# Dynamic convolution and two dense layers on one core: 24 shared 4 KB places and a written-out order of issue

## The chip, the cores and the metric

The kernel runs on one core of one Trainium2 chip. The metric is the device time of one execution in microseconds (us). Engines are named as in the profile: PE multiplies matrices (PEld loads its weights), DVE, ACT and POOL work on tiles elementwise, SP only issues DMAs. SBUF is the on-chip memory of the tiles, PSUM the small one that PE writes.

## The reference

```python
w = softmax(weight_gen over its 7 taps)                       # 2 x 4096 x 8 x 7
x1[s, h, :] = sum over k of w[s, h, k] * x[s + k - 6, h, :]   # 8 heads of 24 columns
h = x1 @ w_in;  g = h / (1 + exp(-h));  x2 = g @ w_out        # 8192x192 -> 2048 -> 192
h = x2 @ w_in2
g = (a0 + a1*h + a2*h^2 + a3*h^3) / (1 + |b0|*|h| + |b1|*h^2 + 1e-6)
out = g @ w_out2
```

All of it in float32. The weights arrive as 8-byte floats and are turned into 4-byte ones on the chip, with integer operations on their two words.

## The kernel before

**Tiling.** The 8192 tokens are cut into 16 blocks of 512. A block goes through the convolution (`attention`, four token groups j), a transpose on PE (T), the first layer in eight units u of 256 hidden columns (`unit1`), a step between the layers (`between`), the second layer in eight units (`unit2`), and `finish`, which transposes back and stores.

**Two halves for each operand.** PE's fast float32 format keeps fewer bits, so each operand is split into a rounded half (hi) and the rest (lo = value - hi). A group of ten 512-column matmuls makes one hidden tile `h` (A in layer 1, B in layer 2: `mm1`, L544), another group of ten adds the unit to the output (C, D: `mm2`, L565 to L569). The second operand halves are `xh`, `xl` (inputs of a layer), `g1h`, `g1l`, `g2h`, `g2l` (activated hidden tiles).

**Chains of a unit.** Layer 1: A, then on ACT the silu in place (S, L581) and the rounded half (H, L585), then on DVE the lo subtraction (L, L589). Layer 2: B, then on ACT two readers of the PSUM tile (U, L626 and V, L630), then on DVE u (L636) and w (L639), which read the PSUM tile too, and Y (L645); on ACT a logarithm and a sigmoid (N, L650 and G, L653), which make the reciprocal; on DVE the product g (L656); the rounded half h (L243 on ACT, L245 on POOL or L247 on DVE) and the lo subtraction l (L666, on DVE or POOL), which read and write SBUF alone. S, N and G need three different function tables on ACT, so a change among them costs an ACT_TABLE_LOAD.

**PSUM** holds two `h` tiles (also used by T and by the transpose back, FT), and the two accumulators. A group A or B starts when the tile two before it has been read for the last time: by L in layer 1, by w in layer 2.

**Order.** Every operation has a number in the table KEYS (one table for blocks 0, 1 and 15, one for the rest, moved by 72 a block); `Plan.order` sorts all 2922 of them, and each engine executes its own in that order, one after another. ENGINES picks another engine for some. SBUF tiles come from pools with a fixed number of buffers, taken in turn: five `y`, five `t` (both serve as raw and decoded weights during the start), two each of `g1h`, `g1l`, `g2h`, `g2l`, one of each other. In the convolution, M multiplies 7 taps by their weights, p, r and a add them up, AD copies a part of the result by DMA (L493), and `between` swaps two halves by DMA.

Of the kernel before, what the change touches and what calls it, by code (L numbers as in the profile page):

```python
# [17 lines left out]
P = 128  # L18
J = 64
JB = 4  # L20
# [16 lines left out]
PERIOD = 72.0  # L37
KEYS = """
    q0O0l:-3113.02 q0O2l:-2632.43 q0B0l:-2598.9 q0O2a:-2459.82 q0A0l:-2443.19 q0O6l:-2381.11 q0A0a:-2309.74
    q0O21:-2304.16 q0A01:-2174.4 q0O0a:-2166.02 q0B0a:-2153.38 q0O22:-2115.39 q0B01:-2103.18 q0B02:-1964.9  # L40
    q0B03:-1964.37 q0O23:-1909.62 cn:-1901.54 q0B04:-1854.81 s0l:-1796.69 q0O01:-1778.45 q0O24:-1772.97 q0O02:-1754.69
    q0O2h:-1739.82 q0B0d:-1736.66 q0A02:-1725.96 q0A1l:-1702.71 q0B0h:-1658.16 q0O03:-1644.78 q0O04:-1637.27
    q0A03:-1622.71 q0O0h:-1589.04 q0O6a:-1548.27 q0A04:-1539.2 q0A3l:-1532.67 q0O2x:-1506.98 q0A0h:-1485.47
    q0O61:-1471.06 q0O62:-1222.76 s0m:-1222.04 q0O63:-1184.06 q0O64:-1181.21 q0A0x:-1178.74 q0B1l:-1155.86
    q0O3l:-1152.08 zX:-1141.9 q0O6h:-1137.28 q0O0x:-1127.08 q0O6x:-1123.86 q0A1a:-1119.13 q0O3a:-1106.14
    q0A3a:-1087.37 q0A11:-1077.61 q0A31:-1051.29 q0O31:-1041.27 q0O1l:-1030.01 q0B0x:-1018.44 s0e:-1007.59
    q0B1a:-1005.54 q0A32:-994.85 s0n:-994.421 q0O32:-983.167 q0O1a:-945.552 q0A12:-913.372 q0A33:-900.533
    q0A13:-897.059 q0A34:-892.163 q0B11:-885.891 q0A14:-877.139 zM0:-874.91 q0O11:-866.459 zp0:-861.802 q0B12:-857.071
# [36 lines left out]
    q1O44:27.349 H5:27.354 yL0:28.011 zB2:28.845 q1O5x:29.2 L5:29.276 zU0:31.816 zu0:33.193 A7:34.231 q1O1x:34.79
    zV2:35.354 C5:37.242 S7:37.852 H7:38.496 q1O4h:38.505 zw0:40.456 C6:40.558 zU2:41.599 zV0:42.24 zY2:42.469
# [71 lines left out]
def table(text, kind):  # L158
    return {n: kind(v) for n, v in (e.split(":") for e in text.split())}
# [602 lines left out]
```

## Time and profile before

| what | value |
|---|---|
| median of 3 runs | 1366.06 us (1366.05 to 1366.27) |
| profiled execution, first to last instruction (span) | 1361.5 us |
| the runs' median less that span | 4.56 us |
| busy: PE, ACT, DVE, POOL | 91%, 88%, 84%, 34% |

The span is read as a start (decoding weights, first blocks), a steady part in which a block takes 77.8 us, and an end in which the last block has nothing to overlap with. A busy time counts instructions that overlap once.

### The profile page before, as it was taken

To read this page: it belongs to the slowest core of one execution; us is meant where nothing else is said; L and a number is where in the kernel's file an instruction comes from. 1 tells how busy PE (TensorE), PEld (TensorE's weight loads), DVE (VectorE), ACT (ScalarE), POOL (GpSimd) and SP (SyncE) were. 2 spreads that over 40 slices of the span, in tenths; PEclk is the share of its full clock that TensorE was granted. 3 is DMA by queue.
4 is the path that set the end of the run, shared out by engine and by line. 5 is a ranking of instruction groups with operands and counts; after the bars stand their busy time and mean duration, and the time that the engine had idled before them with its cause. 6 is when DMAs were issued, how large, how long until landed. Compare 5 with 4: busy or idle time off the path is not lost.

```text
span 1361.5 us, 14596 instructions
## 1 busy us (share of the span) xinstructions
PE 1243.2 (91%) x5440; PEld 990.5 (73%) x5440; DVE 1147.1 (84%) x1128; ACT 1192.4 (88%) x1129; POOL 468.5 (34%) x260
## 2 busy tenths in 40 slices
PE   0269899999999999999999999999999999999986
PEld 0147678777777877777877877787787777777764
DVE  5988888798889888788887998888888888878896
ACT  2375999989899998989999898989999898999996
POOL 0013534343524335252534425253443525211111
PEclk9989999999999999999999999999999999999999
DMA  6641011001011100101010100101010010000000
GB/s 182 185 144 56 14 43 37 20 0 37 20 51 40 37 20 2 36 20 37 20 37 20 49 34 8 37 20 37 20 37 20 1 37 20 5 20 0 20 1 24
DMA packets 26855, 49.20 MB, mean 36 GB/s; under 512 B 10916, under 2 KB 17186, under 8 KB 26784
## 3 DMA queue, kind: packets, MB, share of 16 engines
q1 hardware_dynamic: 26784, 48.27, 11.8%
q8 instruction: 43, 0.70, 0.2%
q14 instruction: 28, 0.23, 0.1%
HBM read 31.86 MB, written 8.01 MB: 29 GB/s over the span
## 4 chain that ended last, share of the span: by engine, by line
ACT 50%; PE 27%; DVE 12%; issue 7%; DMA 2%; SPq 0%; POOLq 0%; POOL 0%; ACTq 0%; DVEq 0%
PE h L544 17%; ACT y L650 7%; ACT L581 6%; ACT t L626 6%; ACT h L581 6%; ACT y L653 6%; ACT g1h L585 5%; ACT y L630 5%; ACT L650 4%; DVE g1l L589 4%; ACT L653 3%; PE acc L569 2%; PE acc L565 2%; PE acc L568 2%; PE acc L566 2%
## 5 line engine op out<-in xcount | busy, mean ns | idle before, releaser
L544 PE MATMUL h<-xh,wa 128*128 128x512 f32 x1024 | 332.1, 406 | 49.2 <-DVE g1l L589 32.5
L544 PEld LDWEIGHTS h<-xh,wa 128*128 128x128 f32 x1024 | 184.6, 190 | 127.1 <-DVE g1l L589 56.3
L589 DVE TENSOR_TENSOR g1l<-h,g1h 128x1024 fp32r<-128x1024 f32 x128 | 156.5, 1224 | 117.1 <-ACT g1h L585 115.9
L464 POOL TENSOR_TENSOR pr<-xw,aw 128x1344 f32<-128x1344 f32 x56 | 176.2, 3146 | 208.5 <-DVE ao L483 205.2
L245 POOL TENSOR_SCALAR g2h<-t 128x1024 fp32r<-128x1024 f32 x77 | 94.0, 1221 | 353.7 <-PE acc L567 254.8
L544 PE MATMUL h<-xl,wa 128*128 128x512 f32 x512 | 202.3, 395 | 0.9 <-DVE xl L521 0.8
L544 PE MATMUL h<-xh,wb 128*128 128x512 f32 x512 | 202.1, 395 | 0.0
L544 PE MATMUL h<-xl,wb 128*128 128x512 f32 x512 | 201.5, 394 | 0.0
L656 DVE SCALAR_TENSOR_TENSOR t<-t,a_sb,y 128x1024 f32<-128x1024 f32 x128 | 166.1, 1301 | 18.7 <-ACT y L653 18.7
L626 ACT ACTIVATE t<-h,a_sb 128x1024 f32<-128x1024 f32 x128 | 153.7, 1201 | 27.2 <-PE h L544 26.2
L581 ACT ACTIVATE h<-h 128x1024 f32<-128x1024 f32 x128 | 129.2, 1010 | 52.0 <-PE h L544 41.9
L645 DVE SCALAR_TENSOR_TENSOR y<-y,b_sb 128x1024 f32<-128x1024 f32 x128 | 168.2, 1314 | 7.6 <-ACT y L630 4.8
L639 DVE SCALAR_TENSOR_TENSOR t<-t,a_sb,h 128x1024 f32<-128x1024 f32 x128 | 163.7, 1279 | 2.9
L636 DVE TENSOR_TENSOR t<-t,h 128x1024 f32<-128x1024 f32 x128 | 155.6, 1216 | 11.0 <-ACT y L630 5.2
L630 ACT ACTIVATE y<-h,b_sb 128x1024 f32<-128x1024 f32 x128 | 141.7, 1107 | 8.5 <-PE h L544 7.0
L650 ACT ACTIVATE y<-y,c_sb 128x1024 f32<-128x1024 f32 x128 | 142.5, 1148 | 2.8 <-DVE y L645 1.8
L666 DVE TENSOR_TENSOR g2l<-t,g2h 128x1024 fp32r<-128x1024 f32 x92 | 139.8, 1522 | 2.6 <-POOL g2h L245 2.5
L585 ACT ACTIVATE g1h<-h 128x1024 fp32r<-128x1024 f32 x128 | 131.1, 1025 | 4.7 <-PE acc L567 1.3
L666 POOL TENSOR_TENSOR g2l<-t,g2h 128x1024 fp32r<-128x1024 f32 x36 | 89.5, 2487 | 131.5 <-DVE g2h L247 130.2
L653 ACT ACTIVATE y<-y 128x1024 f32<-128x1024 f32 x128 | 130.4, 1056 | 0.7
L544 PEld LDWEIGHTS h<-xl,wa 128*128 128x128 f32 x512 | 97.4, 190 | 23.7 <-DVE xl L521 2.3
L544 PEld LDWEIGHTS h<-xh,wb 128*128 128x128 f32 x512 | 97.4, 190 | 21.4
(94 smaller groups left out, 2452.8 us busy)
## 6 DMA issues: line engine op xcount, KB each, us to landing
xw<-in_x_dram SPq DMA_DIRECT2D x14, 960.0 KB, 5.1
raw<-in_moe_w_out_dram SPq DMA_DIRECT2D x16, 384.0 KB, 4.1
out_dram<-of SPq DMA_DIRECT2D x16, 384.0 KB, 2.3
raw<-in_moe_w_in_dram SPq DMA_DIRECT2D x8, 512.0 KB, 5.7
e<-e SPq DMA_DIRECT2D x32, 128.0 KB, 2.3
raw<-in_moe_w_in_dram SPq DMA_DIRECT2D x8, 256.0 KB, 6.1
dup<-dec SPq DMA_DIRECT2D x16, 128.0 KB, 2.3
ao<-ao SPq DMA_DIRECT2D x16, 128.0 KB, 2.3
```

What stands on the lines that cost most here:

```text
L464: e.tensor_tensor(out=p.rearrange("p k (h g) -> p k h g", g=G), in0=st[xw][:, j:j + K, :].rearrange("p k (h g) -> p k h g", g=G), in1=weig ...
L544: pe.matmul(out=h[:, i], lhsT=w[:, f], rhs=xx, start=(n == 0), stop=(n == len(terms) - 1))
L581: act.activation(out=st[hb], in_=st[hb], func=AF.Silu)
L585: act.activation(out=t, in_=st[hb], func=AF.Copy)
L589: dve.tensor_tensor(out=t, in0=st[hb], in1=st[gh].bitcast(F32), op=ALU.subtract)
L626: act.activation(out=q, in_=st[hb], func=AF.Identity, scale=a_sb[:, 3:4], bias=a_sb[:, 2:3])
L630: act.activation(out=q, in_=st[hb], func=AF.Abs, scale=b_sb[:, 1:2])
L645: dve.scalar_tensor_tensor(out=st[y], in0=st[y], scalar=b_sb[:, 0:1], in1=st[y], op0=ALU.add, op1=ALU.mult)
L650: act.activation(out=st[y], in_=st[y], func=AF.Ln, scale=c_sb[:, 0:1], bias=1e-6)
L653: act.activation(out=st[y], in_=st[y], func=AF.Sigmoid, scale=-1.0)
L656: dve.scalar_tensor_tensor(out=st[t], in0=st[t], scalar=a_sb[:, 0:1], in1=st[y], op0=ALU.add, op1=ALU.mult)
L666: e.tensor_tensor(out=q, in0=st[t], in1=st[gh].bitcast(F32), op=ALU.subtract)
```

## The change

1. **Places.** The pools of `y`, `t`, `g1h`, `g1l`, `g2h`, `g2l`, `xh`, `xl`, `ao` and `of` (24 buffers in all) become 24 single buffers named a to x. The order names the place of each new tile (`H1.5:r`).
2. **Order.** KEYS and ENGINES go; ORDER lists all 2922 operations, each block with an order of its own, with the choice of engine (`@1`).
3. **Engines.** By that list: of the 128 lo subtractions of layer 2, 84 run on POOL (36 before); of the 128 rounded halves 9 run on ACT (30 before), 32 on DVE (21) and 87 on POOL (77); of the copies out of PSUM in `finish` DVE makes 15 of 16 FE (none before) and 7 of 16 FC (1), ACT the others; of the 192 additions p, r, a 141 run on POOL (58 before), of the 64 products M 43 (56 before).
4. **AD** becomes a copy on POOL (12 blocks) or ACT (2), and stays a DMA in 2.
5. ACT and DVE read one PSUM tile one after the other; the list gives the turn per unit (V, U, u, w or U, V, u, w in 120 of 128 units, V behind u in the others; before 125). The arithmetic is the same.

```diff
-BUFS = dict(
-    h=2, acc0=1, acc1=1, xw=1, aw=2, pr=1, ao=1, xh0=1, xl0=1, xh1=1, xl1=1, of=1,
-    g1h=2, g1l=2, y=5, t=5, g2h=2, g2l=2,
-)
...
+    r0.3@1 L1.2:x A2.2 G7.0 a0.3:i M2.3 g7.0 B0.1 S2.2 H2.2:r p2.3@1 C1.2 U0.1:b L2.2:t V0.1:v q1O72 r2.3@1 A3.2
...
+SLOTS = "abcdefghijklmnopqrstuvwx"
+SHARED = {"y", "t", "g1h", "g1l", "g2h", "g2l", "ao", "of", "xh0", "xl0", "xh1", "xl1"}
+OWN = dict(xw=1, pr=1, aw=2)
...
+            for v in bufs:
+                if v[0] in SHARED and v not in self.slot:
+                    self.slot[v] = slot
+            fn(engines[names[int(e or 0)]])
...
-    def new(tag, shape, dt=F32, name=None):
-        return sb.tile(shape, dt, tag=tag, name=name or tag, bufs=BUFS[tag])
+    def new(buf, shape, dt=F32, name=None):
+        if buf[0] in SHARED:
+            return sb.tile(shape, dt, tag="s" + plan.slot[buf], name=name or buf[0], bufs=1)
+        return sb.tile(shape, dt, tag=buf[0], name=name or buf[0], bufs=OWN[buf[0]])
...
-            sp.dma_start(out=t[:, :, D:2 * P], in_=t[:, :, P:D])
+            if e is sp:
+                sp.dma_start(out=t[:, :, D:2 * P], in_=t[:, :, P:D])
+            else:
+                round_to(e, t[:, :, D:2 * P], t[:, :, P:D])
...
-        plan.op("AD", b, "SP", dup, rd=at, wr=at)
+        plan.op("AD", b, "POOL ACT DVE SP", dup, rd=at, wr=at)
```

**What moves, place 1.** SP's queue from the start: `raw` is an undecoded weight chunk, `dup<-dec` a copy that waits until a chunk has been decoded, `xw` the convolution's input. Before, then now:

```order
L346 DMA raw<-in_moe_w_out_dram 128x2x384 x2
L344 DMA raw<-in_moe_w_in_dram 64x1024 x2
L340 DMA raw<-in_moe_w_in_dram 128x1024
L346 DMA raw<-in_moe_w_out_dram 128x2x384
L294 DMA aw<-in_weight_gen_dram 128x224
L383 DMA dup<-dec 64x512 x4
L340 DMA raw<-in_moe_w_in_dram 128x1024 x2
L344 DMA raw<-in_moe_w_in_dram 64x1024 x2
```

```order
L400 DMA raw<-in_moe_w_out_dram 128x2x384
L394 DMA raw<-in_moe_w_in_dram 128x1024
L400 DMA raw<-in_moe_w_out_dram 128x2x384
L398 DMA raw<-in_moe_w_in_dram 64x1024 x2
L400 DMA raw<-in_moe_w_out_dram 128x2x384
L348 DMA aw<-in_weight_gen_dram 128x224
L400 DMA raw<-in_moe_w_out_dram 128x2x384 x2
L394 DMA raw<-in_moe_w_in_dram 128x1024
L437 DMA dup<-dec 64x512 x4
```

Eight chunks (nine DMAs) stand ahead of the copy that waits, where five chunks (six DMAs) stood before.

**Place 2.** POOL's queue in the steady part: `pr` and `ao` belong to the convolution, `g2h` is a rounded half, `g2l` a lo subtraction. Before (blocks 6 to 11 read alike), then now, in the middle of block 8's second layer:

```order
L464 TENSOR_TENSOR pr<-xw,aw 128x1344
L473 TENSOR_TENSOR pr<-pr 128x576
L464 TENSOR_TENSOR pr<-xw,aw 128x1344
L245 TENSOR_SCALAR g2h<-t 128x1024
L666 TENSOR_TENSOR g2l<-t,g2h 128x1024
L464 TENSOR_TENSOR pr<-xw,aw 128x1344
L473 TENSOR_TENSOR pr<-pr 128x576
L464 TENSOR_TENSOR pr<-xw,aw 128x1344
L245 TENSOR_SCALAR g2h<-t 128x1024
L477 TENSOR_TENSOR pr<-pr 128x384
L483 TENSOR_TENSOR ao<-pr 128x192
```

```order
L518 TENSOR_TENSOR pr<-xw,aw 128x1344
L527 TENSOR_TENSOR pr<-pr 128x576
L531 TENSOR_TENSOR pr<-pr 128x384
L537 TENSOR_TENSOR ao<-pr 128x192
L297 TENSOR_SCALAR g2h<-t 128x1024
L723 TENSOR_TENSOR g2l<-t,g2h 128x1024
L297 TENSOR_SCALAR g2h<-t 128x1024
L723 TENSOR_TENSOR g2l<-t,g2h 128x1024
L297 TENSOR_SCALAR g2h<-t 128x1024
L723 TENSOR_TENSOR g2l<-t,g2h 128x1024
L297 TENSOR_SCALAR ao<-ao 128x4x64
```

Lo subtractions stand in runs, each behind its rounded half, and the sums of a product follow it on the same engine.

**Place 3.** ACT's queue just ahead of the transposed input of block 9 (`xh<-tp`): `y<-y,c_sb` is the logarithm, `y<-y` the sigmoid, `h<-h` the silu. Before, then now:

```order
L650 ACT_TABLE_LOAD
L650 ACTIVATE y<-y,c_sb 128x1024 x2
L581 ACT_TABLE_LOAD
L581 ACTIVATE h<-h 128x1024
L653 ACT_TABLE_LOAD
L653 ACTIVATE y<-y 128x1024
L585 ACTIVATE g1h<-h 128x1024
L243 ACTIVATE of<-to 128x768
L650 ACT_TABLE_LOAD
L650 ACTIVATE y<-y,c_sb 128x1024
L517 ACTIVATE xh_5021<-tp 128x1024
```

```order
L707 ACT_TABLE_LOAD
L707 ACTIVATE y<-y,c_sb 128x1024 x3
L638 ACT_TABLE_LOAD
L638 ACTIVATE h<-h 128x1024
L642 ACTIVATE g1h<-h 128x1024
L710 ACT_TABLE_LOAD
L710 ACTIVATE y<-y 128x1024 x2
L574 ACTIVATE xh_5056<-tp 128x1024
```

Three logarithms share a table where two and one did, so one load goes; the copy `of<-to` has left the engine. Over the program ACT has 203 table loads, 214 before.

## Rows read from the trace of the kernel before

**Rows 1.** The page: span, then busy time of each engine with instructions.
```profile
span 1361.5 us, 14596 instructions
PE 1243.2 (91%) x5440; PEld 990.5 (73%) x5440; DVE 1147.1 (84%) x1128; ACT 1192.4 (88%) x1129; POOL 468.5 (34%) x260
```
**Rows 2.** Stretches: length, busy us (instructions) by engine, PE's granted clock, DMA share, GB/s.
```profile
0.00:61.60 61.60, 4.14 (x11) 2.27 (x11) 46.83 (x100) 19.07 (x31) 3.69 (x11) 1.00 0.61 171
61.60:118.40 56.80, 42.79 (x163) 33.56 (x162) 49.66 (x78) 31.62 (x39) 9.52 (x12) 0.88 0.44 131
118.40:192.50 74.10, 66.91 (x282) 52.44 (x281) 61.53 (x72) 66.47 (x63) 33.23 (x23) 0.98 0.14 42
192.50:348.00 155.50, 149.99 (x666) 120.00 (x665) 130.00 (x119) 144.74 (x134) 64.06 (x34) 1.00 0.08 25
348.00:1203.00 855.00, 838.76 (x3720) 672.18 (x3719) 734.10 (x660) 794.30 (x739) 331.24 (x163) 1.00 0.08 26
656.50:734.30 77.80, 76.60 (x342) 61.41 (x341) 65.99 (x60) 72.20 (x68) 30.52 (x16) 1.00 0.08 25
1203.00:1361.50 158.50, 140.59 (x607) 110.06 (x605) 124.97 (x105) 136.22 (x126) 26.72 (x18) 0.97 0.04 14
```
**Rows 3.** The page: the chain that ended last, share of the span by engine.
```profile
ACT 50%; PE 27%; DVE 12%; issue 7%; DMA 2%; SPq 0%; POOLq 0%; POOL 0%; ACTq 0%; DVEq 0%
```
**Rows 4.** Waits in one steady block, 656.5 to 734.3: us in total, times, longest.
```profile
ACT h L581 <- PE h L544: 2.8, 2, 2.1
PEld h L544 <- DVE g1l L589: 2.7, 4, 0.9
```
**Rows 5.** Timeline of DVE in the start: start us, us, instruction, [idle before, releaser].
```profile
5.98 0.36 DVE L357 TENSOR_SCALAR dec<-dec 128x384 f32<-128x384 f32 x1 [5.98 <-ACT dec L353]
10.06 0.43 DVE L357 TENSOR_SCALAR dec<-dec 128x512 f32<-128x512 f32 x1 [3.72 <-ACT dec L353]
...
26.87 0.69 DVE L357 TENSOR_SCALAR dec<-dec 128x512 f32<-128x512 f32 x2 [2.70 <-ACT dec L353]
```
**Rows 6.** Timeline of SP's queue in the start.
```profile
13.76 2.42 SPq L383 DMA_DIRECT2D dup<-dec  x4
16.30 1.00 SPq L340 DMA_DIRECT2D raw<-in_moe_w_in_dram  x2
```
**Rows 7.** Line L243 on ACT: durations in ns, min/median/max.
```profile
L243 ACT ACTIVATE g2h<-t x30: 1052/1063/1074, 200.1 to 1340.7; 128x1024 fp32r<-128x1024 f32 x30
...
L243 ACT ACTIVATE of<-to x16: 792/804/810, 261.3 to 1357.3; 128x768 f32<-128x768 f32 x16
L243 ACT ACTIVATE of<-acc x15: 1015/1018/1024, 325.7 to 1354.7; 128x1024 f32<-128x1024 f32 x15
```
**Rows 8.** Groups by line: busy us, mean ns | idle before, releasers.
```profile
L666 DVE TENSOR_TENSOR g2l<-t,g2h 128x1024 fp32r<-128x1024 f32 x92 | 139.8, 1522 | 2.6 <-POOL g2h L245 2.5
L581 ACT ACT_TABLE_LOAD x78 | 100.1, 1283 | 1.8 <-PE h L544 0.4
L666 POOL TENSOR_TENSOR g2l<-t,g2h 128x1024 fp32r<-128x1024 f32 x36 | 89.5, 2487 | 131.5 <-DVE g2h L247 130.2
L464 DVE TENSOR_TENSOR pr<-xw,aw 128x1344 f32<-128x1344 f32 x8 | 12.5, 1558 | 2.5 <-DMA aw<-wsm 2.4
```
**Rows 9.** Convolution's `pr` alone over the program: DVE, POOL busy us (instructions).
```profile
0.00:1361.50 1361.50, 84.93 (x142) 266.54 (x114) 0.99 0.12 36
```
**Rows 10.** Line L247 on DVE: durations in ns, min/median/max.
```profile
L247 DVE CAST g2h<-t x21: 682/695/698, 158.9 to 1315.8; 128x1024 fp32r<-128x1024 f32 x21
...
L247 DVE COPY of<-acc x1: 1218/1218/1218, 241.6 to 241.6; 128x1024 f32<-128x1024 f32 x1
```
**Rows 11.** Timeline of 673 to 692: lo subtractions on DVE, a product on POOL.
```profile
673.92 3.54 POOL L464 TENSOR_TENSOR pr<-xw,aw 128x1344 f32<-128x1344 f32 x1 [3.07 <-DVE ao L483]
...
676.08 2.45 DVE L666 TENSOR_TENSOR g2l<-t,g2h 128x1024 fp32r<-128x1024 f32 x1
...
691.39 1.22 DVE L666 TENSOR_TENSOR g2l<-t,g2h 128x1024 fp32r<-128x1024 f32 x1
```

More of the change, by code (lines that the diff above doesn't have):

```diff
@@ L179, in op, with run @@
             need.update(self.readers.pop(t, ()))
-            self.writer[t] = n
-        need.discard(n)
-        own = {t[:-1] for t in (*rd, *wr) if t[0] in BUFS}
-        for v in own:
-            self.users.setdefault(v, []).append(n)
-        own_key = "" if name[0] in "qsc" else {0: "z", 1: "y", NB - 1: "e"}.get(b, "")
-        name = own_key + name
-        engines = engines.split()
-        eng = engines[self.engines.get(name, 0)]
-        key = self.keys.get(name, 0.0) + (0.0 if own_key else b * PERIOD)
-        self.ops.append((key, name, b, engines, eng, fn, need, own))
-    def order(self):
-        order = sorted(range(len(self.ops)), key=lambda i: (self.ops[i][0], i))
-        place = {i: n for n, i in enumerate(order)}
-        for i in order:
-            late = [self.ops[j][1:3] for j in self.ops[i][6] if place[j] > place[i]]
-            assert not late, (self.ops[i][1:3], "before", late)
-        return order
+            self.writer[t] = name
+        need.discard(name)
+        bufs = []
+        for t in (*wr, *rd):
+            if t[:-1] not in bufs:
+                bufs.append(t[:-1])
+        assert name not in self.ops
+        self.ops[name] = (engines.split(), fn, need, bufs)
+    def run(self, engines):
+        done = set()
+        for entry in ORDER.split():
+            head, _, slot = entry.partition(":")
+            name, _, e = head.partition("@")
+            names, fn, need, bufs = self.ops[name]
+            assert need <= done and name not in done, name
+            done.add(name)
+            for v in bufs:
+                if v[0] in SHARED and v not in self.slot:
+                    self.slot[v] = slot
+            fn(engines[names[int(e or 0)]])
+        assert len(done) == len(self.ops)
 @with_exitstack
@@ L219 @@
     sb = ctx.enter_context(tc.tile_pool(name="sb", bufs=1))
-    hp = ctx.enter_context(tc.tile_pool(name="hp", bufs=BUFS["h"], space=PSUM))
+    hp = ctx.enter_context(tc.tile_pool(name="hp", bufs=2, space=PSUM))
     ap1 = ctx.enter_context(tc.tile_pool(name="ap1", bufs=1, space=PSUM))
@@ L379, in double @@
         def double(e):
-            st[dup] = t = new("t", [P, W2], name="dup")
+            st[dup] = t = new(dup, [P, W2], name="dup")
             for i in range(2):
@@ L729 @@
     with tc.manual_schedule():
-        for i in plan.order():
-            plan.ops[i][5](engines[plan.ops[i][4]])
+        plan.run(engines)
 _INS = ['x', 'weight_gen', 'moe_w_in', 'moe_w_out', 'moe2_w_in', 'moe2_w_out', 'moe2_a', 'moe2_b']
```

337 lines of the change are left out of this document (194 added, 143 removed).

## The prediction

> **What bounds the kernel now.** I read the page's busy times first [rows 1], then the stretches [rows 2], then the chain that ended last [rows 3] and the waits of one steady block [rows 4]. The busy times name no single limit: PE 91%, ACT 88%, DVE 84%. The stretches do. Their cuts lie where a block's transposed input is split (348 is block 4, 1203 block 15), so that they hold equal work.
>
> - 0 to 61.6: DVE decodes weights and runs the first convolution, 100 instructions in 46.83 us; the other 14.8 us it is idle. PE has done next to nothing.
> - 61.6 to 118.4: DVE is still the fullest, 49.66 of 56.8 us. PE's granted clock averages 0.88, so some matmuls run at the lower of its two levels, 1.2 GHz instead of 2.4.
> - 118.4 to 192.5: ACT is the fullest, 66.47 of 74.1.
> - 192.5 to 348: PE 149.99 and ACT 144.74 of 155.5.
> - 348 to 1203, eleven blocks of 77.7 us: PE is busy for 838.76 of 855 us (98%), at full clock. ACT has 93%, DVE 86%, POOL 39%. The steady part is bound by PE, and all that can be won there without fewer matmuls is PE's idle time, 16.2 us.
> - From 1203: 158.5 us, in which PE idles 18 and ACT 22.
>
> Half of the chain is ACT's [rows 3], though PE is the fuller in the steady part. The waits show why both appear: in one block ACT's silu waits 2.8 us for a group of matmuls, and PE's first weight load of a group 2.7 us for the lo subtraction that frees a PSUM tile [rows 4]. The two engines hand two PSUM tiles back and forth, and DVE stands in that loop.
>
> **The change, part by part.** The sum is made against the profiled execution, 1361.5 us of span [rows 1]; the median of the runs, 1366.06, is 4.56 more, which I carry over.
>
> *ACT.* It loses 21 rounded halves of 1.063 us (22.3), 15 copies of 0.804 (12.1), 6 of 1.018 (6.1) [rows 7] and 11 table loads of 1.283 [rows 8] (14.1): 54.6. It gains two copies for AD and some five of weights, under 1 us each; I take 3.6. So 1192 falls to 1141 us. None of this is on the path by itself where PE is full; it shortens the loop where ACT is late.
>
> *DVE.* It loses 48 lo subtractions at 1.522 [rows 8], 73.1. Of its convolution work, 84.93 us in 142 instructions [rows 9], 72 stay: 21 products at 1.558 [rows 8] and 51 additions, whose mean is (84.93 - 12.5)/134 = 0.54, together 60.3, so 24.6 less. It gains 11 rounded halves of 0.695 (7.6), 6 copies of 1.218 (7.3) [rows 10] and 15 of 768 columns, which no row shows on DVE: between those two, 0.95 (14.3). Net -68.5, so 1147 falls to about 1079.
>
> *POOL.* 48 lo subtractions at 2.487 [rows 8] add 119 us; 70 more of the convolution's, at most at the mean of 266.54/114 = 2.34 [rows 9], 164 at most. So POOL goes from 468 to between 588 and about 770, at most 57% of the span. It is hidden as long as nothing waits for one of its results.
>
> *The start.* Five weight chunks are asked for at once; the next load is issued at 16.30, behind the copies at 13.76 that wait for decoded data [rows 6], and DVE waits 2.70 us for it at 26.87 [rows 5]. Now eight chunks go out ahead of that copy, so this wait should go, and part of the 3.72 before 10.06; the first 5.98 stays. I take 4 of the 14.8 idle us, between 0 and 8. Ahead of the first split input DVE has 92 instructions instead of 100, and 67 instead of 76 up to the second. At the stretch's mean of 46.83/100 [rows 2] these are 3.7 and 4.2; both lie on the path, because DVE is the fullest engine there. Up to the third, ACT has nine table loads instead of thirteen (5.1 us) but more other work (1.6), and one group of matmuls slips behind the stretch: 3 of the 3.5 count. From 192.5 to 348 PE is full, and that group comes back: 0. AD's copy no longer goes through SP's queue; its landing time is covered, since DVE has ten other instructions (4.7 us at the mean above) between the last addition and the split. **Start: -4 - 3.7 - 4.2 - 3 = -15**, between -4 and -24.
>
> *The steady part.* The order moves no matmuls across its ends (352 groups in both). ACT gets about 3 us a block free, and by the list a place has been read for the last time at least two groups of matmuls before its next tile, where pools of two tied a rounded half to one particular group. Both shorten the loop of rows 4. I take 9 of PE's 16.2 idle us, between 0 and 14.
>
> *The port.* The trace has a price for DVE and POOL at the same time. A lo subtraction of DVE, 1.22 us at 691.39, takes 2.45 at 676.08, while a product on POOL takes 3.54 [rows 11]; and the group's mean is 1.522 [rows 8]. The excess, 92 x 0.30 = 28 us, is on DVE now. With half as many such subtractions there but some 1.5 times the POOL time, it is of the same size, 14 to 40 us, and spread over 16 blocks. DVE has 86% in the steady part, so most is absorbed; I charge +3 on the path, between 0 and +40 (the rival below).
>
> The Trainium skill ("SBUF — State Buffer", Who interferes with whom) speaks against this change: a DVE instruction with two SBUF inputs and a GpSimd instruction that reads SBUF exclude each other for a whole instruction, and the later one blocks fully. The rows agree with the size (1.23 us added, about what is left of a POOL instruction). By it the work that needs the port in a block has to fit end to end into 77 us, and it would do so, so the sum stays as it is; what the rule threatens is the order of arrival.
>
> *The end.* The last block has as much ACT work as before, and one matmul group more behind the last hidden tile (2.3 us), against FE and FC off ACT. I take 0, between -6 and +6.
>
> **Sum:** -15 - 9 + 3 + 0 = -21, span 1340.5, time **1345 us**.
>
> **The rivals.**
>
> *A. The port turns it slower* (the rule above, priced by rows). Each steady block gets 3 more lo subtractions and 4.4 more additions on POOL. If DVE meets each once and loses the 1.23 us of rows 11, that is 9.1 us a block. DVE, 65.99 of 77.8 [rows 2] less 4.3 plus 9.1, would still fit. But DVE executes in order, and behind a blocked instruction stands the lo subtraction that frees a PSUM tile. If a third of it reaches PE, it is 3 us a block, 39 over 13 blocks: 1345 + 39 = **1384 us**. It decides from about 1.5 us a block on, where the start's gain is eaten. For it: DVE is already late for PE [rows 4]. Against it: before, the same collision cost DVE 28 us and PE next to nothing, 98% busy.
>
> *B. Only the start gains.* PE at 98% is PE at its end; the 16 us are the filling after each small wait and stay. Then -15 + 3: **1354 us**. This lies in the forecast's own range.
>
> *C. It doesn't show.* If the loads are not what the start waits for, and DVE's saving turns into waits for ACT, the start gives 2 to 4 us and the port takes them: **1365 us**.
>
> *D. More.* All of the idle time goes (-14), and the start gives -24: **1326 us**.
>
> **How the numbers follow.** About 0.2% (2.7 us) can be told from no change. The forecast with B (1335 to 1358): 0.58. D: 0.14. C: 0.10, most of it within 0.2%. A: 0.18, a little of which ends within 0.2%. So faster 0.75, same 0.08, slower 0.17. The range reaches from a little below D to where a mild A begins, 1322 to 1372, and leaves out 0.18, mostly A's upper part.
>
> **What would show it.** Right: table loads 203; DVE's first split input at about 53 instead of 61.6, block 4's near 332; PE's clock above 0.88 in the second stretch; eleven steady blocks in 840 to 850 us, with PE idle for less than 16. ACT near 1141, DVE near 1080, POOL 590 to 770. Wrong: steady blocks of 78 us or more, lo subtractions on DVE above the 1.522 of now, and PE's waits for the layer-1 lo subtraction above 2.7 us a block would be A; a first split input still at 60 would be C.

## The result, and the profile after

| | before | after |
|---|---|---|
| runs, median (us) | 1366.05 (1363.32 to 1366.27, 4 runs) | 1322.79 (1322.34 to 1323.87, 4 runs) |
| profiled execution, span | 1361.5 | 1320.6 |

The ratio is 0.9691, 95% interval [0.9677, 0.9704]: the change makes the kernel faster by 43.3 us, where 21 were predicted. The direction was right and the time lies inside the range, but the gain is twice the forecast. Of the 43.3 us, 40.9 lie between the two spans. The other 2.4 come from which executions were profiled. A run's time is some 1.8 us more than its span; beyond that, the execution profiled before (1363.32) ran 2.7 us under its median, and that of after (1322.34) 0.45. The prediction carried 4.56 over as if all of it belonged to the kernel.

The page of after, against [rows 1] and [rows 3]:

```profile
span 1320.6 us, 14524 instructions
PE 1226.7 (93%) x5440; PEld 992.5 (75%) x5440; DVE 1126.2 (85%) x1034; ACT 1147.1 (87%) x1083; POOL 669.4 (51%) x403
...
PE 59%; ACT 16%; DVE 14%; issue 6%; DMA 2%; POOL 1%; SPq 1%; ACTq 0%; POOLq 0%; DVEq 0%
```

The chain that ended last ran half on ACT before; now it runs mostly on PE. That is the better answer to [rows 3] than the busy shares: the program is now held by its matmuls more than by what comes between them.

The stretches of after, cut where the input of block 0, 1, 2, 4 and 15 is split (the columns are those of [rows 2]):

```profile
0.00:54.10 54.10, 3.98 (x10) 2.28 (x11) 43.96 (x92) 18.84 (x31) 3.43 (x11) 1.00 0.90 237
54.10:102.20 48.10, 42.82 (x163) 33.38 (x162) 46.33 (x68) 33.20 (x44) 12.13 (x15) 0.93 0.45 134
102.20:172.50 70.30, 62.99 (x272) 49.21 (x271) 62.16 (x69) 61.78 (x60) 43.83 (x30) 1.00 0.08 22
172.50:324.30 151.80, 150.43 (x682) 123.77 (x681) 135.42 (x117) 142.66 (x131) 94.48 (x57) 1.00 0.07 21
324.30:1173.80 849.50, 832.06 (x3725) 677.95 (x3724) 717.31 (x587) 761.03 (x702) 473.29 (x270) 1.00 0.08 25
1173.80:1320.60 146.80, 134.38 (x597) 105.94 (x595) 120.99 (x107) 129.63 (x119) 42.25 (x22) 0.99 0.05 15
```

And of before. In [rows 2] the cuts at 348 and 1203 lie 1.1 us behind the split of block 4 and 3.1 us ahead of that of block 15, so a steady block takes 78.1 us and not 77.7:

```profile
192.40:346.90 154.50, 148.99 (x662) 119.16 (x661) 129.04 (x118) 143.76 (x133) 64.06 (x34) 1.00 0.08 25
346.90:1206.10 859.20, 842.96 (x3742) 675.73 (x3742) 736.54 (x661) 798.45 (x743) 331.24 (x163) 1.00 0.09 26
1206.10:1361.50 155.40, 137.49 (x589) 107.42 (x587) 123.59 (x103) 133.16 (x123) 26.72 (x18) 0.97 0.04 12
```

Part by part, with the term of the prediction beside it:

| part | before | after | change | predicted |
|---|---|---|---|---|
| to the first split input | 61.6 | 54.1 | -7.5 | -7.7 |
| to block 1's | 56.8 | 48.1 | -8.7 | -4.2 |
| to block 2's | 74.0 | 70.3 | -3.7 | -3 |
| to block 4's | 154.5 | 151.8 | -2.7 | 0 |
| eleven steady blocks | 859.2 | 849.5 | -9.7 | -9 + 3 |
| the end | 155.4 | 146.8 | -8.6 | 0 |
| profiled execution against median | | | -2.4 | 0 |

The prediction took the parts to hold equal work; they don't quite. By PE's records (x, transposes with them) the third has 10 fewer, the fourth 20 more, the steady part 17 fewer and the end 8 more. At the fourth part's 149 / 662 = 0.225 us a record, an estimate, the fourth part gained some 7 us for equal work, where the predicted 0, with one group of ten coming back, makes 2.3; and over 2 of the third part's 3.7 us are matmuls that moved on.

So the misses are the end (8.6), the second part (4.5), the steady part (3.7), the fourth part (2.7) and the execution that was profiled (2.4).

Where PE's weight loads wait in the eleven steady blocks, before and then after (us, times, longest):

```profile
PEld h L544 <- DVE g1l L589: 32.2, 44, 1.6
PEld h L544 <- issue: 10.2, 31, 0.5
PEld h L544 <- ACT y L630: 4.0, 9, 0.5
```

```profile
PEld h L601 <- issue: 9.0, 13, 1.5
PEld h L601 <- DVE g1l L646: 4.1, 7, 1.3
PEld acc L625 <- DVE g1l L646: 3.6, 3, 2.3
PEld tp L557 <- DVE g1l L646: 2.9, 3, 1.5
```

The wait for layer 1's lo subtraction (`g1l`), four times a block before [rows 4], is the one that shrank: 32.2 us to 10.6 over three lines.

The same view of PE's matmuls while the pipeline fills (50 us to block 4's split input), before, then after:

```profile
PE h L544 <- DVE g1l L589: 17.9, 8, 7.5
PE tp L500 <- DVE ao L483: 8.9, 2, 5.0
PE h L544 <- DVE t L639: 5.5, 6, 1.6
```

```profile
PE h L601 <- DVE g1l L646: 6.3, 6, 2.5
PE h L601 <- DVE t L696: 4.7, 5, 2.0
PE acc L622 <- ACT g1h L642: 2.2, 1, 2.2
```

Here too the subtraction, and with it the convolution's last addition (`ao`), for which the transposes waited 8.9 us and now do not.

The port between DVE and POOL, which the largest rival feared, shows in the groups by line (busy us, mean ns | idle before):

```profile
L723 POOL TENSOR_TENSOR g2l<-t,g2h 128x1024 fp32r<-128x1024 f32 x84 | 219.7, 2619 | 134.5 <-DVE g2h L299 86.7 <-issue 18.5 <-ACT g2h L295 15.8
L702 DVE SCALAR_TENSOR_TENSOR y<-y,b_sb 128x1024 f32<-128x1024 f32 x128 | 191.8, 1506 | 13.7 <-ACT y L687 13.6
L713 DVE SCALAR_TENSOR_TENSOR t<-t,a_sb,y 128x1024 f32<-128x1024 f32 x128 | 178.7, 1408 | 26.1 <-ACT y L710 26.1
L696 DVE SCALAR_TENSOR_TENSOR t<-t,a_sb,h 128x1024 f32<-128x1024 f32 x128 | 163.8, 1280 | 5.8 <-ACT y L687 1.8
L723 DVE TENSOR_TENSOR g2l<-t,g2h 128x1024 fp32r<-128x1024 f32 x44 | 64.0, 1454 | 0.7
```

Line L702 (Y) and line L713 (the product g) had a mean of 1314 and 1301 ns before, with a median of 1280 both times; 128 x (1506 - 1314) and 128 x (1408 - 1301) are 24.6 and 13.7 us more. All 38 of the Y and all 24 of the g that took over 60 ns more than the median had a POOL instruction running beside them. L696 (w), of the same size but with one input in PSUM, stayed at 1280 ns, though POOL ran beside it too. So the collisions did grow on DVE, in other instructions than those that the prediction watched, and the kernel is faster all the same.

### The profile page after: what moved, and what is told of

Read it like the earlier page. It is cut to its first block, busy times and chain, and to the rows that moved or that the text cites. A ratio compares the mean times of both kernels' runs of the same rounds, so it can differ in the third digit from the quotient of the medians.

```text
span 1320.6 us, 14524 instructions
## 1 busy us (share of the span) xinstructions
PE 1226.7 (93%) x5440; PEld 992.5 (75%) x5440; DVE 1126.2 (85%) x1034; ACT 1147.1 (87%) x1083; POOL 669.4 (51%) x403
## 4 chain that ended last, share of the span: by engine, by line
PE 59%; ACT 16%; DVE 14%; issue 6%; DMA 2%; POOL 1%; SPq 1%; ACTq 0%; POOLq 0%; DVEq 0%
PE h L601 31%; PE acc L625 5%; PE acc L626 5%; PE acc L622 5%; PE acc L623 5%; PE acc L624 5%; DVE t L693 3%; DVE t L696 2%; ACT y L707 2%; ACT y L687 2%; ACT t L683 2%; ACT L638 2%; ACT h L638 2%; ACT g1h L642 2%; DVE y L702 2%
## 5 line engine op out<-in xcount | busy, mean ns | idle before, releaser
L601 PE MATMUL h<-xh,wa 128*128 128x512 f32 x1024 | 324.8, 399 | 28.2 <-DVE t L696 16.5
L723 POOL TENSOR_TENSOR g2l<-t,g2h 128x1024 fp32r<-128x1024 f32 x84 | 219.7, 2619 | 134.5 <-DVE g2h L299 86.7
L297 POOL TENSOR_SCALAR g2h<-t 128x1024 fp32r<-128x1024 f32 x87 | 113.8, 1310 | 275.6 <-DVE t L713 243.3
L601 PEld LDWEIGHTS h<-xh,wa 128*128 128x128 f32 x1024 | 188.6, 190 | 86.1 <-issue 15.7
L646 DVE TENSOR_TENSOR g1l<-h,g1h 128x1024 fp32r<-128x1024 f32 x128 | 156.3, 1221 | 62.2 <-ACT g1h L642 57.6
L702 DVE SCALAR_TENSOR_TENSOR y<-y,b_sb 128x1024 f32<-128x1024 f32 x128 | 191.8, 1506 | 13.7 <-ACT y L687 13.6
L713 DVE SCALAR_TENSOR_TENSOR t<-t,a_sb,y 128x1024 f32<-128x1024 f32 x128 | 178.7, 1408 | 26.1 <-ACT y L710 26.1
L696 DVE SCALAR_TENSOR_TENSOR t<-t,a_sb,h 128x1024 f32<-128x1024 f32 x128 | 163.8, 1280 | 5.8 <-ACT y L687 1.8
L683 ACT ACTIVATE t<-h,a_sb 128x1024 f32<-128x1024 f32 x128 | 153.5, 1200 | 11.6 <-PE h L601 11.3
L518 POOL TENSOR_TENSOR pr<-xw,aw 128x1344 f32<-128x1344 f32 x43 | 121.5, 2826 | 47.1 <-DVE ao L537 43.6
L527 POOL TENSOR_TENSOR pr<-pr 128x576 f32<-128x576 f32 x50 | 91.3, 1825 | 65.6 <-DVE pr L518 63.3
```

What stands on the lines that cost most here:

```text
L601: pe.matmul(out=h[:, i], lhsT=w[:, f], rhs=xx, start=(n == 0), stop=(n == len(terms) - 1))
L646: dve.tensor_tensor(out=t, in0=st[hb], in1=st[gh].bitcast(F32), op=ALU.subtract)
L683: act.activation(out=q, in_=st[hb], func=AF.Identity, scale=a_sb[:, 3:4], bias=a_sb[:, 2:3])
L696: dve.scalar_tensor_tensor(out=st[t], in0=st[t], scalar=a_sb[:, 1:2], in1=flat(), op0=ALU.add, op1=ALU.mult)
L702: dve.scalar_tensor_tensor(out=st[y], in0=st[y], scalar=b_sb[:, 0:1], in1=st[y], op0=ALU.add, op1=ALU.mult)
L713: dve.scalar_tensor_tensor(out=st[t], in0=st[t], scalar=a_sb[:, 0:1], in1=st[y], op0=ALU.add, op1=ALU.mult)
```

## The experiments

A kernel's list names an operation, its engine (`@1`: the second one that the operation may use) and its tile's place (`:k`). Unless it says "own places", an experiment's places were given anew, each new tile getting the one that had been free longest; the ninth run is the control for that. The parts of each profiled execution, in us (1 to 4 are the first four of the table above):

| kernel | 1 | 2 | 3 | 4 | steady | end | runs' median |
|---|---|---|---|---|---|---|---|
| before | 61.6 | 56.8 | 74.0 | 154.5 | 859.2 | 155.4 | 1366.05 |
| after | 54.1 | 48.1 | 70.3 | 151.8 | 849.5 | 146.8 | 1322.79 |
| e1_places | 61.7 | 59.1 | 76.8 | 154.1 | 859.8 | 154.8 | 1370.29 |
| e2_start | 55.2 | 47.6 | 71.6 | 151.8 | 860.9 | 154.5 | 1343.36 |
| e3_end | 61.6 | 57.4 | 79.3 | 154.1 | 860.0 | 147.2 | 1361.63 |
| e4_lo_back | 56.1 | 48.2 | 71.9 | 153.2 | 878.2 | 157.2 | 1363.08 |
| e5_act_back | 53.6 | 48.2 | 73.0 | 162.0 | 867.9 | 155.1 | 1361.08 |
| e6_ad_dma | 55.5 | 50.0 | 73.2 | 154.3 | 850.3 | 146.6 | 1332.33 |
| e7_lo_alone | 61.5 | 56.6 | 76.5 | 155.5 | 868.0 | 157.9 | 1380.47 |
| e8_engines_alone | 62.7 | 55.1 | 77.5 | 162.5 | 900.4 | 165.5 | 1425.70 |
| e9_places_lru | 54.3 | 48.7 | 71.9 | 151.7 | 849.8 | 146.5 | 1324.24 |
| e10_five | 59.7 | 47.3 | 71.3 | 151.7 | 848.8 | 147.9 | 1329.18 |
| e11_m01 | 54.3 | 51.6 | 71.7 | 151.8 | 847.2 | 147.8 | 1326.24 |
| e12_ad_own | 54.5 | 51.9 | 73.0 | 154.3 | 850.6 | 146.6 | 1331.17 |
| e13_end_lo | 54.9 | 47.1 | 72.8 | 151.7 | 847.0 | 158.1 | 1331.83 |
| e15_ad_alone | 65.3 | 57.4 | 74.1 | 154.5 | 859.1 | 155.3 | 1364.45 |
| e16_ten | 62.2 | 47.5 | 70.3 | 151.8 | 849.2 | 146.5 | 1327.10 |

The kernel before had a median of 1364.7 to 1365.4 beside the experiments, so ratios to it are given where a per cent matters.

### Places, and which part gains by the order

**e1_places.** The list of the change is replaced by the order and the engines of before, with places:

```diff
-    M0.8 ... r0.8@1 ... M2.8@1 ... r2.8@1
+    M0.8 ... r0.8 ... M2.8 ... r2.8
...
-    h1.8:n ... l1.8@1:l ... h3.8:c
+    h1.8@2:o ... l1.8@1:g ... h0.8@1:a
```

> The order and the engines of the kernel before, with the 24 shared places of the change (each new tile gets the place that has been free longest). Theory ORDER (the gain comes from the written order, part by part; which buffer a tile takes matters little): 1364 to 1368 us, as before. Theory PLACES (pools that take turns kept tiles waiting for one particular buffer; that loss is what I mis-sized in the end and the steady part): steady blocks shorter by up to 0.9 us each and an end shorter by up to 8, so 1346 to 1356.

Measured: ratio 1.0037 [1.0025, 1.005]. Shared places alone gain nothing; steady part and end are those of before within 0.6 us, and the second and third part are together 5 us longer, which is why the time lies above ORDER's figure too. PLACES falls.

**e2_start** and **e3_end.** The list is cut and joined at one operation:

```diff
-    h4.2:c XL0.4:e M2.5 C7.3 G6.2 V7.2:m
+    h4.2:w C7.3 XL0.4:b A0.4 O.1 G6.2
```

(e2; up to here the list of the change, from here that of before. e3 is the other way round, joined at `XL0.15`.)

> The list of the change up to block 4's first split input, then the order and engines of before, all in shared places. Theory ORDER: the start's gain alone, by the traces 22.6 us of it, so block 4's split input near 324 us (347 before) and 1341 to 1347 in all, the steady part at 858 to 860 us and the end at 154 to 156. Theory PLACES: 1325 to 1333, since the steady part and the end gain as well. My prediction's sizes (start -15): 1351.

> The order and engines of before up to block 15's first split input, then the list of the change, all in shared places. Theory ORDER with an end that gains by itself (what the two traces show, -8.6): 1356 to 1359. My prediction's end of 0 (and the 8.6 in the trace would be work that the earlier parts had already moved ahead): 1364 to 1368. Theory PLACES: 1346 to 1351.

Measured: 0.9839 [0.9826, 0.9853] and 0.9976 [0.9967, 0.9986]. e2 has the start of after within 1.3 us a part and the steady part and end of before. e3 has the steady part of before, a third part 5.3 us longer, and an end of 147.2 us, as after; against e1, whose start is as long to within 0.7 us, it gains 1370.29 - 1361.63 = 8.7 us. So start and end gain by their own pieces of the list, and the end's 8.6 us are its own, not work that earlier parts had taken over. The steady part's piece was not run alone. Of the 46.1 us between e1 and e9 (below) the two leave 10.5 for it, and its stretch is 10.0 shorter. In the third expectation I had forgotten what the places would cost the start, so the total alone lies between its figures; the part decides.

### Order without the engines, engines without the order

**e4_lo_back.**

```diff
-    l0.8@1 ... l2.8@1 ... l5.8@1 ... l6.8@1
+    l0.8 ... l2.8 ... l5.8 ... l6.8
```

> The order of the change, with the lo subtractions of layer 2 on the engines of before (36 on POOL instead of 84). DVE's work grows by about 48 x 1.5 = 73 us. Theory RELIEF (the steady part gains because DVE is relieved of subtractions): the steady part's 9.7 us go and the end's as well, 1333 to 1345. Theory ORDER (DVE at 85% has room, POOL's collisions get rarer by as much): 1321 to 1327, with the subtraction on DVE near 1.5 us.

Measured: 0.999 [0.9981, 0.9999]. Moving the subtractions back takes 40 of the 43 us. ORDER falls as I had put it, and RELIEF is too small as well, so the run missed both: the steady part is 878.2 us, 19 longer than that of before itself. Its stretch, and PE's waits in it:

```profile
329.40:1207.60 878.20, 840.27 (x3726) 680.58 (x3725) 762.17 (x625) 761.99 (x702) 377.76 (x231) 0.99 0.08 24
```

```profile
PE h L678 <- DVE t L773: 16.3, 23, 2.9
PE h L678 <- DVE g1l L723: 8.3, 9, 1.9
```

DVE is busy for 762 of 878 us (87%), far from full, but late at the reads that free a PSUM tile (`t`, `g1l`). In the trace of after the same two waits are 7.7 and 1.7 us.

**e5_act_back.**

```diff
-    h1.8 ... h5.8@2 ... FC.8@1 ... FE.8@1
+    h1.8@2 ... h5.8@1 ... FC.8 ... FE.8
```

> The order of the change, with FE, FC and the rounded halves h on the engines of before (ACT takes 15 FE, 6 FC and 21 halves more, about 40 us). After the subtractions of layer 2 turned out to be worth 40 us in this order, theory ALL ENGINES (order and engines belong together, each shift of work back costs) expects the same sort of loss here: 1340 to 1365, most of it in the steady part. Theory ACT HAS ROOM (in the changed kernel ACT has 761 of 849.5 us in the steady part, so 40 us over 16 blocks, 2.5 a block, fit into its idle time): 1321 to 1330.

Measured: 0.9974 [0.9965, 0.9982], a loss of 38 us, as ALL ENGINES had it, though only half of it (18.4 us) is in the steady part; the fourth part loses 10.2 and the end 8.3. ACT has room by its busy time (784.58 of 867.9 us in the steady part) and the loss is there all the same.

**e7_lo_alone** and **e8_engines_alone**, both on e1:

```diff
-    l0.8 ... l2.8 ... l5.8 ... l6.8
+    l0.8@1 ... l2.8@1 ... l5.8@1 ... l6.8@1
```

> The order of before (in shared places, 1370 with the engines of before), with layer 2's lo subtractions on the engines of the change (84 on POOL). Theory RELIEF ALONE (DVE's 73 us less are what the steady part and the end gain from): the steady part loses 8 to 15 us and the end 5 to 8, 1345 to 1358. Theory JOINT (a list fits its own engines; POOL's late halves and products now stand behind subtractions of 2.5 us each): no gain or a loss, 1366 to 1400.

> The order of before in shared places, with every choice of engine of the change (layer 2's subtractions and halves, FE, FC, the convolution, AD). RELIEF ALONE: at least what the subtractions alone give, 1335 to 1355. JOINT: 1366 to 1420, since POOL gets some 200 us of work at places in its order where others wait for it.

Measured: 1.0114 [1.01, 1.0128] and 1.0452 [1.0437, 1.0466]. Against e1 the subtractions alone cost 10 us and all engines together 55, 6 more than JOINT's upper figure. PE's wait for DVE in the steady part of e1:

```profile
PE h L678 <- DVE g1l L723: 13.4, 33, 1.2
```

Of e8's waits in the steady part, PE's and then DVE's:

```profile
PE h L678 <- DVE g1l L723: 23.6, 33, 3.1
PE h L678 <- DVE t L773: 13.8, 27, 0.9
PE acc L702 <- DVE g1l L723: 9.5, 5, 4.2
```

```profile
DVE of L376 <- PE to L828: 37.3, 11, 4.9
```

Four times lie side by side: old order and old engines 1370, new order with old subtractions 1363, old order with all new engines 1426, both new 1323. It is not a full square, since the new order with all the old engines was not run. JOINT stands as far as these go: the new engines without the order lose, the new order without its engine for the subtractions loses nearly all of its gain; a list is made for its engines. It also bears on rival A of the prediction. E8 has the loss which A described, DVE late for PE, but not by A's cause alone: DVE, in its own order, stands for 37.3 us at the copies `of` that it took over (FE), waiting for PE's transposes back, a wait that e1 doesn't have. How much of the loss is the port is not shown.

**e9_places_lru**, the control: the change's list, only the letters behind the colons differ.

```diff
-    h1.8:n ... l1.8@1:l
+    h1.8:k ... l1.8@1:j
```

> The order and engines of the change, word for word, with the 24 places given anew (each new tile the place that has been free longest, as in the runs on parts of the change so far). This is the control for those runs. If the choice of place matters little: 1321 to 1326, and the losses of the runs with engines moved back are the engines' own. If the change's own choice of places carries part of its gain (the order of before lost 5 us in the first blocks with places given this way): 1327 to 1335, in the start's parts, and as much is to be taken off those losses.

Measured: 0.9703 [0.969, 0.9716] against 0.9691 [0.9677, 0.9704]: no difference that can be told. The losses of e4, e5 and e6 are the engines' own.

### The start

**e6_ad_dma** and **e12_ad_own** (own places):

```diff
-    AD.0@1 ... AD.1@1 ... AD.3 ... AD.8
+    AD.0@3 ... AD.1@3 ... AD.3@3 ... AD.8@3
```

> The order of the change, with AD by DMA in all blocks. My prediction priced AD's copy at nothing (ten other DVE instructions cover the landing): 1322 to 1325. If AD's landing is what the split input waits for in the start, up to 2 us in each of the first blocks: 1326 to 1332, in the start's parts.

> The change with its own places, AD by DMA in all blocks. With the run that had AD by DMA and other places at 1332: theory LANDING (the copy's transfer is late for the split input): 1328 to 1333 again, with waits of DVE or PE for it in the first blocks. Theory PLACES (those 9.5 us were the places): 1322 to 1325.

Measured: 0.9764 [0.9751, 0.9778] and 0.9756 [0.9743, 0.977], so 8 to 9 us more than after with either places, nearly all of it in the second, third and fourth part (3.8, 2.7 and 2.5 us in e12). PE's waits from 50 us to block 4's split input in e12:

```profile
PE tp L636 <- DMA ao<-ao: 7.1, 3, 4.2
PE h L678 <- DVE g1l L723: 6.1, 6, 2.1
```

The transposes wait 7.1 us for the transfer, three times. LANDING stands.

**e15_ad_alone**: the kernel before, with the AD edit and nothing else.

```diff
...
-        plan.op("AD", b, "SP", dup, rd=at, wr=at)
+        plan.op("AD", b, {0: "ACT", 1: "ACT", 2: "SP", 15: "SP"}.get(b, "POOL"), dup, rd=at, wr=at)
```

> The kernel before with one edit: AD as a copy on ACT (2 blocks) or POOL (12), as in the change, its own pools and order. In the changed order AD by DMA cost 8.4 us. Theory ORDER MAKES IT (before, PE waits for this transfer for only 1.9 us, because T stands far behind AD): 1362 to 1366. Rival (the landing time is on the path in the old order as well): 1355 to 1360.

Measured: 1.0 [0.9991, 1.0009]. In the old order the transfer was covered (PE waited 1.9 us for it in the trace of before), so the same edit is worth nothing there and 8 us in the new one. The edit removes what the new order would have exposed. (The profiled execution ran 3.0 us above the median; its first part, 65.3 us, has a wait of 5.04 us for a weight chunk, 2.70 in before.)

**e10_five** (own places):

```diff
-    q0O3l s0l q0O4l q0O2a q0O6l q0O21 q0A1l ... q0B0d q0O32
+    q0O3l s0l q0O2a q0O21 ... q0B0d q0O4l q0O6l q0A1l q0O32
```

> The change with its own places; three of the eight weight chunks ahead of the first waiting copy in SP's queue are asked for behind it, so that five stand ahead, as before. My prediction's term (4 us of the start's gain come from there): 1325 to 1329, the first part 57 to 60 us instead of 54.1. Rival (DMA engines, not the queue's order, set the landing, or DVE has other chunks to decode): 1322 to 1325.

Measured: 0.9741 [0.9728, 0.9754], 6.4 us more; the first part is 59.7 instead of 54.1. DVE's waits in the timeline, e10 and then after (start us, us, instruction, [idle before]):

```profile
10.25 0.43 DVE L488 TENSOR_SCALAR dec<-dec 128x512 f32<-128x512 f32 x1 [0.41 <-ACT dec L484]
19.61 0.36 DVE L488 TENSOR_SCALAR dec<-dec 128x384 f32<-128x384 f32 x1 [3.54 <-ACT dec L484]
```

```profile
4.79 0.36 DVE L411 TENSOR_SCALAR dec<-dec 128x384 f32<-128x384 f32 x1 [4.79 <-ACT dec L407]
11.11 0.43 DVE L411 TENSOR_SCALAR dec<-dec 128x512 f32<-128x512 f32 x1 [1.17 <-ACT dec L407]
```

With five chunks ahead of the copy DVE waits 3.54 us at 19.61 for a chunk, as in before it waited 2.70 for another at 26.87 [rows 5]; with eight, the longest wait for a chunk between 12 and 40 us is 0.55. The term held. What the prediction left in place, the first wait of 5.98 us, is 4.79 in after: a smaller chunk is asked for first.

**e16_ten** (own places):

```diff
-    q0B04 q0B0d q0O32 ... X.0 ... q0A3l q0O1l
+    q0B04 X.0 q0A3l q0O1l q0B0d q0O32
```

> The change with its own places and two more weight chunks and the convolution's first input ahead of the first waiting copy in SP's queue (ten chunks instead of eight). Five instead of eight cost 6.4 us. If the landing of loads still holds DVE up (it waits 0.85 us for the input at 23.3 and 0.55 at 29.5 for a chunk): 1320 to 1322. If the eight have taken all there is, or the DMA engines are shared by more: 1322 to 1325.

Measured: 0.9723 [0.971, 0.9736], 4.3 us more than after: a miss, outside both figures. Not only two chunks went ahead, but also the convolution's input (`X.0`, some 950 KB). The copy that waits on decoded data now stands behind so many loads that its own transfers are late. SP's queue in e16, what it waited for, and the waits of ACT and DVE:

```profile
15.51 6.80 SPq L514 DMA_DIRECT2D dup<-dec  x4
```

```profile
SPq L514 <- DMA raw<-in_moe_w_in_dram: 2.6, 1, 2.6
SPq L514 <- DMA xw<-in_x_dram: 2.1, 1, 2.1
```

```profile
31.12 1.06 ACT L372 ACTIVATE wb<-dup 128x1024 fp32r<-128x1024 f32 x1 [11.18 <-DMA dup<-dec]
```

```profile
32.21 1.22 DVE L541 TENSOR_TENSOR wb<-dup,wb 64x1024 fp32r<-64x1024 f32 x1 [10.65 <-ACT wb L372]
```

and the same copy in after:

```profile
13.97 2.42 SPq L437 DMA_DIRECT2D dup<-dec  x4
```

The row of 6.80 us holds four issues, each as short as in after, and 4.7 us in which SP waits for earlier loads to land. The copy's first piece then lands 14.2 us after its issue (the median of these copies is 2.3), ACT waits 11.18 us for it and DVE 10.65 for ACT. So eight is a number that fits, not the first step of a trend; which of the three loads did the harm is not shown.

**e11_m01** (own places): the store of the softmax weights and the load of block 1's later, block 1's first product on DVE.

```diff
-    L1.0 s1s X.1 ... q0O4h AW.1 ... M0.1@1
+    L1.0 X.1 ... s1s ... H3.0 AW.1 ... M0.1
```

> The change with its own places; in the second part of the start the store of the softmax weights and the load of block 1's are issued as late as before, and block 1's first product M goes back to DVE. Theory IDLE (the step that my sum missed in this part is DVE's own waiting, 2.4 us of it for this load): the second part 48.1 grows by 2.4 to 4.5, 1325 to 1328. Rival (DVE waits for the hi half at the part's end anyway, and the product's time is only shifted): 1322 to 1324.

Measured: 0.9721 [0.9708, 0.9734], 3.5 us more, all of it in the second part. The size is that of IDLE, the place is not: DVE does not wait for the load, as it did before (2.40 us at 93.83), but for a product on POOL that comes late:

```profile
86.34 1.00 DVE L604 TENSOR_TENSOR pr<-pr 128x576 f32<-128x576 f32 x1 [4.37 <-POOL pr L595]
```

So waiting of this sort in the second part is worth its price in time. That the load's wait in particular gave 2.4 of the 8.7 us is not shown.

### The end

**e13_end_lo** (own places): from block 15's split input on, the subtractions on the engines of before. Nine differ: seven go from POOL to DVE, four of them in block 14, and two of block 15 from DVE to POOL.

```diff
-    l0.14@1 ... l6.14@1 ... l5.14@1 ... l7.14@1 ... l0.15@1 ... l2.15@1
+    l0.14 ... l6.14 ... l5.14 ... l7.14 ... l0.15 ... l2.15
```

> The change with its own places; from block 15's split input on, layer 2's lo subtractions on the engines of before (9 operations differ: 6 of blocks 13, 14 and 15 go from POOL to DVE, one more of block 15, two of block 15 the other way). Theory RELIEF AT THE END (DVE's subtractions of block 14, which overlap with the last block's first layer, are what the end term of my prediction left out): the end 146.8 grows to 151 to 156, 1326 to 1332 in all. Rival (the end gains by its order and by the clock that follows from it): at most 2 us, 1322 to 1325.

Measured: 0.9758 [0.974, 0.9776], 9 us more. The end:

```profile
1173.50:1331.60 158.10, 138.97 (x597) 109.07 (x595) 131.68 (x112) 129.69 (x119) 29.17 (x17) 0.96 0.04 14
```

DVE has 131.68 us of work instead of 120.99, and the part is 11.3 longer, 2 more than expected; PE's granted clock averages 0.96 instead of 0.99. With the same 597 records, PE's idle time has 6.7 of the 11.3 us and its busy time 4.6. RELIEF AT THE END stands, with the clock as its companion: two stretches of the end of before show what a wait costs there.

```profile
1309.00:1312.50 3.50, 3.50 (x10) 2.70 (x9) 3.46 (x4) 3.35 (x4) 1.93 (x1) 0.53 0.02 5
1347.00:1350.50 3.50, 3.50 (x10) 2.27 (x9) 2.42 (x2) 0.84 (x1) 0.89 (x2) 0.59 0.00 0
```

There PE, right after waits of 3.43 us (to 1308.56) and 2.68 us (to 1345.48), ran for some 3 us each near the lower of its two levels, 1.2 GHz. Not every wait is followed by this: after 1.95 us (to 1331.1) in the same end, and 2.06 us (to 1263.8) in that of after, the granted clock stayed at 1.00, the upper level. What PE waits for in the end, before and then after:

```profile
PE acc L568 <- DVE g2l L666: 4.5, 4, 2.7
PE h L544 <- ACT y L630: 3.4, 1, 3.4
```

```profile
PE h L601 <- DVE t L696: 4.1, 6, 2.1
...
PE acc L625 <- DVE g2l L723: 0.3, 1, 0.3
```

The 4.5 us of waiting for DVE's subtractions of layer 2 are down to 0.3. In the end of after the clock is 0.99, and PE is busy 3.1 us less with 8 matmul records more.

## Why the prediction was right and wrong

**Right.** The start's first part: -7.5 against -7.7, with its cause (the chunks ahead of the waiting copy, e10). Its third: -3.7 against -3. The steady part: -9.7 against -6 in all, inside its bounds, by the loop of [rows 4], whose wait fell from 32.2 to 10.6 us; an estimated 2.5 of the 9.7 are 17 fewer matmul records, most of them transposes. Table loads are 203; the convolution's `pr` on DVE is 60.41 us against 60.3; FE's copies measured 0.951 us against an estimated 0.95; PE's clock in the second part is 0.93 against "above 0.88".

**The end, the step that failed worst.** "The last block has as much ACT work as before, and one matmul group more behind the last hidden tile (2.3 us), against FE and FC off ACT. I take 0, between -6 and +6." It asked what the last block does, but the part from 1206 on also holds block 14's second layer, in which four subtractions more go to POOL; and it counted ACT's work, where PE waited longest for DVE's subtractions, one by one (4.5 us in the view above). E13 shows the price of these few operations in the new order, 11.3 us of the end and 9.0 in the runs' medians; with them on DVE the new order's end, 158.1 us, is longer than the old one's 155.4.

**The second part.** "Ahead of the first split input DVE has 92 instructions instead of 100, and 67 instead of 76 up to the second. At the stretch's mean of 46.83/100 [rows 2] these are 3.7 and 4.2; both lie on the path, because DVE is the fullest engine there." The busy time did fall by 3.3 us, but DVE's idle time in that part, 56.8 - 49.66 = 7.14, was left standing without being priced; it became 48.1 - 46.33 = 1.77. For the first part the prediction had priced both kinds of time and was right.

**AD.** "... its landing time is covered, since DVE has ten other instructions (4.7 us at the mean above) between the last addition and the split." This looked at the split on DVE. What waits for AD is the transpose on PE, and e12 shows 7.1 us of it, 8.4 in the runs. The old order covers it, as the trace of before said (1.9 us), and a term of zero read from that order was carried into an order in which it doesn't hold. By size that is most of the 4.5 and 2.7 us by which the second and fourth part were missed. In the second part e11's edits cost 3.5 us as well, so the two shares can't be told apart there.

**Three signs were wrong.** Block 4's split input came at 324.3 us, not near 332: the second and fourth part. I expected PE's idle time in the steady part to fall below 16 us. It is 849.5 - 832.06 = 17.4; the gain lies in PE's busy time, 842.96 to 832.06 (with 17 matmul records fewer), because short waits between matmuls count as busy: from one 512-column matmul's start to the next the median is 227 ns in both, and what lies 5 to 200 ns above 226 adds up to 15.4 us before and 8.4 after. The waits of the weight loads show the gain; the idle time does not. And DVE was to fall to 1080 us; it is 1126. Of these 46 us, 38 are Y and the product g, which meet POOL more often.

**The rivals.** A, the port, is half true: DVE loses more to POOL's instructions than before. The Trainium skill ("SBUF — State Buffer", Who interferes with whom) has a DVE instruction with two SBUF inputs and a POOL instruction that reads SBUF exclude each other; the rows agree (Y's mean 1314 to 1506 ns, its longest 3634, POOL's subtraction 2487 to 2619). But PE's idle time in the steady part is 17.4 us against 16.2, so little of that reached PE; that what PE needs seldom stands behind a blocked instruction is a likely reason, and not shown. B falls with the steady part and the end, which gained too, and C with the whole. D (1326) was nearest in its number, but by luck: it took all of PE's idle time to go, which it did not, and nothing from the end.

## What to carry to other kernels

A change of order is not priced by work per engine: the same engines in the old order cost 55 us, the new order without the subtractions' engine lost 40 of its 43 us, and only both together gave the whole. So a term read as zero ("covered") is zero for the order in which it was read; name who waits for the result in the new order. And price a part's idle time as well as its instructions, at the end of the program above all, where the last blocks overlap in a different way and each wait of PE can cost its clock too.

## What was not expected of the hardware

- **Many loads ahead delay a small copy's landing.** With ten chunks and the convolution's input ahead, the first of four `dup` copies landed 14.2 us after its issue instead of 2.2. In the stretch from 6 to 14 us the DMA share is 0.48 before and 1.05 in after; the two rows:

```profile
6.00:14.00 8.00, 0.00 (x0) 0.00 (x0) 3.92 (x10) 1.65 (x3) 0.00 (x0) 1.00 0.48 144
```

```profile
6.00:14.00 8.00, 0.00 (x0) 0.00 (x0) 6.68 (x17) 3.31 (x6) 0.00 (x0) 1.00 1.05 298
```

So the DMA engines were half idle there before and are full with eight chunks (the share is 1.07 in e16), which fits with more loads not helping.

- **Collisions on the port moved.** Subtractions on DVE became a little faster in the mean (1522 to 1454 ns) when more of them ran on POOL, while two other lines of DVE became slower by 192 and 107 ns.
